# Products with T in seven half products in the FFN chunks of an attention kernel on one core

## The chip, the cores and the metric

The kernel runs on one core of a Trainium2 chip. Time is device microseconds of one launch; the kernel before has a median of 410.5 us over three runs (409.81 to 410.56).

## The reference

```
q_pool = q.reshape(B, H, S // 2, 2, D).mean(axis=3)          # B, H, S, D = 8, 8, 1152, 64
scores = 1 / sqrt(D) * q_pool @ k^T
attn   = softmax(scores)
x      = (attn @ v), heads side by side: 4608 tokens x 512
a, b   = x @ w1, x @ w2                                      # 512 x 1024 each
h      = a * b @ w3                                          # (a * b) @ w3, w3 is 1024 x 1024
out    = h @ w_out                                           # 1024 x 512
```

Since nothing stands between w3 and w_out, the kernel computes T = w3 @ w_out once (1024 x 512) and then (a * b) @ T. Matmuls take float16 and add up in float32; the output is float32.

## The kernel before, in words

**Attention.** The 64 heads go in 32 pairs; the score matrix of all pairs is cut into 324 slots of 512 columns for each head of a pair. A slot is one call of `scores` (L434): TensorE writes a buffer `psc` of two PSUM banks (three such buffers), ScalarE takes the exponential of it in one instruction (L448) into a ring of float16 in SBUF. Three slots make a visit, and there are 108 visits. The second product, probabilities by v, goes in 144 groups (`av_step`, L940; matmuls at L471 and L474), each for 128 pooled queries of one pair, or for the short last tiles of two pairs together. DVE divides by the sum of the row (L495 to L511), and the result is turned into `xT` by TensorE (first 8 pairs and short tiles, `x_turn`) or by a transposing DMA on SP's queue (`x_dma`, L481).

**Chunks of the FFN.** The 4608 tokens make 9 chunks of 512. For chunks 0 to 6 `moe_groups` (L597) yields fills, small portions of TensorE work that are put between the attention's. For each of 8 slices ft of d_ff there are two: the projection with w1 (kept in `asb` by DVE, L610) and that with w2, whose eviction multiplies with `asb` into `gT` (`gate`, L613). Then four fills of double length multiply 128 tokens each of gT with T (8 matmuls of 512 columns, L621); DVE scales the result into `osb` (L630), and a DMA stores it, on GpSimd's queue for chunks 0 to 4, on SP's for 5 and 6. T itself is made by earlier fills (`t_groups`, L544). A fill of length 1 is 8 matmuls of 256 columns or 4 of 512.

A fill writes either the one bank `mo` or one of the three psc buffers, which a slot of scores then has to wait for (`bank`, L536).

**The order.** Engines run their queues in the order of the program. Where fills, AV groups and turns of pairs stand between the visits is worked out when the kernel is built: `_visits` (L184) searches over sequences with a table of costs (`_Plan`, L115). In its sequences A is an AV group, P a turn of a pair, m and s a fill in `mo` or in a psc buffer. Chunk c is released to it once the AV groups that it needs are done (`loose`, L904). After the last visit the remaining AV groups and fills alternate (L985 to L992), with six PSUM banks instead of the psc buffers; then the rest of the fills runs without AV groups (L1013), with `asb` kept by ScalarE. Ahead of this loop, DVE has five small instructions for a check of the row sums (L1004 to L1010).

**Chunks 7 and 8** (`late_chunks`, L683) use Winograd's form of Strassen's method for all their products: a product of two matrices, each cut into 2 x 2 blocks, is made from 7 products of blocks instead of 8, with sums of blocks before and after. The sums of the left and right blocks are made by GpSimd: those of w1 and w2 (8 sums of 128 x 1024) and of T (4 of 128 x 1024) in one burst (`weight_sums`, L649, called at L971 when the last but one pair begins), those of x for chunks 7 and 8 (`x_sums`, L670) after the last AV group.

**GpSimd's queue** holds, per pair, the casts of k, q and v to float16 (`cast_kq`, `cast_v`, called by `prepare`, L878, two pairs ahead), the stores of most chunks, and loads of the first pairs. **SP's queue** holds the loads of later pairs, the transposing DMAs and the stores of chunks 5 and 6, in 24 pieces for the latter. At the start 33 matmuls on the identity (L859) run on TensorE before the first data is there.

Of the kernel before, what the change touches and what calls it, by code (L numbers as in the profile page):

```python
# [183 lines left out]
def _visits(n, start, units, pairs, fills, free, ready, width):  # L184
# [8 lines left out]
    for vis in range(n):  # L193
# [12 lines left out]
        def step(p, seq, na, f, pr, t0):  # L206
# [14 lines left out]
            if f < loose:  # L221
                for b in "ms":
                    q = p.copy()
                    q.fill(fills[f][0], fills[f][1], b == "s")
                    step(q, seq + b, na, f + 1, pr, t0)
# [40 lines left out]
def kernel(  # L266
# [26 lines left out]
    QM = 4  # L293
# [250 lines left out]
    def t_groups():  # L544
        w3T = {}

        def turn(ft):
            def go(pt):
                w3T[ft] = msb.tile([128, NF, 128], FP16, tag="w3T", bufs=2, name="w3T")
# [22 lines left out]
    CH = 512  # L572

# [22 lines left out]

    def moe_groups(c):  # L597
        t = {}

# [12 lines left out]
        for ft in range(NF):  # L612
            def gate(pb, ft=ft):  # L613
                nc.vector.tensor_tensor(out=t["g"][:, ft, :], in0=pb, in1=t["a"], op=ALU.mult)  # L614

            yield 1, lambda pa, ft=ft: first(pa, ft), keep, 0.0
            yield 1, lambda pb, ft=ft: proj(pb, w2sb, ft, c), gate, 0.0
        for tt in range(0, CH, 128):
            def go(po, tt=tt):
                for ft in range(NF):  # L620
                    nc.tensor.matmul(po, t["g"][:, ft, tt:tt + 128], T16[:, ft, :],  # L621
                                     start=(ft == 0), stop=(ft == NF - 1))

            def put(po, tt=tt):
                osb = msb.tile([128, dm], FP32, tag="osb", bufs=3)
                if tail[0]:
                    nc.vector.tensor_scalar_mul(out=osb[:, 0:256], in0=po[:, 0:256], scalar1=1.0 / (SCL * SCL))
                    nc.scalar.mul(out=osb[:, 256:512], in_=po[:, 256:512], mul=1.0 / (SCL * SCL))
                else:
                    nc.vector.tensor_scalar_mul(out=osb, in0=po, scalar1=1.0 / (SCL * SCL))  # L630
                if c == LATE - 1:
                    cut = 128 if tt < 256 else 64
                    for r in range(0, 128, cut):
                        for n in range(0, dm, 128):
                            store(nc.sync, c * CH + tt, osb[r:r + cut, n:n + 128], slice(n, n + 128), slice(r, r + cut))
                else:
                    store(nc.sync if c == LATE - 2 else nc.gpsimd, c * CH + tt, osb)

            yield 2, go, put, 0.0

    HF, HM, HC = NF // 2, dm // 2, CH // 2
    LATE = B * Sq // CH - 2
    IS = 1.0 / (SCL * SCL)
    wS, tS, xS = [], {}, {}
# [4 lines left out]
    def weight_sums():  # L649
        for w, tag in ((w1sb, "kst"), (w2sb, "vst")):  # L650
# [4 lines left out]
            nc.gpsimd.tensor_tensor(out=s1, in0=a21, in1=a22, op=ALU.add)  # L655
            minus(s2, s1, a11)
            minus(s3, a11, a21)
            minus(s4, a12, s2)
            wS.append({1: a11, 2: a12, 3: s4, 4: a22, 5: s1, 6: s2, 7: s3})
        b11, b12 = T16[:, 0:HF, 0:HM], T16[:, 0:HF, HM:dm]  # L660
        b21, b22 = T16[:, HF:NF, 0:HM], T16[:, HF:NF, HM:dm]
        st = [att.tile([128, 2, HF, HM], FP16, tag="qst", name="tS") for _ in range(2)]
        t1, t2, t3, t4 = st[0][:, 0], st[0][:, 1], st[1][:, 0], st[1][:, 1]
        minus(t1, b12, b11)
        minus(t2, b22, t1)
        minus(t3, b22, b12)
        minus(t4, b21, t2)
        tS.update({1: b11, 2: b21, 3: b22, 4: t4, 5: t1, 6: t2, 7: t3})

    def x_sums():  # L670
        st = msb.tile([128, 2, 4, NC // 2, HC], FP16, tag="wo", bufs=1, name="xS")
        for c in (0, 1):
            (_, a, n), = runs(LATE + c)
            b11, b12 = xT[:, 0:NC // 2, a:a + HC], xT[:, 0:NC // 2, a + HC:a + n]
            b21, b22 = xT[:, NC // 2:NC, a:a + HC], xT[:, NC // 2:NC, a + HC:a + n]
            x1, x2, x3, x4 = (st[:, c, i] for i in range(4))
            minus(x1, b12, b11)
            minus(x2, b22, x1)
            minus(x3, b22, b12)
            minus(x4, b21, x2)  # L680
            xS[c] = {1: b11, 2: b21, 3: b22, 4: x4, 5: x1, 6: x2, 7: x3}
# [149 lines left out]
    def fill(scored=False):  # L831
# [3 lines left out]
        pt = bank(scored) if put else None  # L835
        go(pt)
        if put:
            put(pt)
# [20 lines left out]
    for _ in range(33):  # L859
        nc.tensor.matmul(avb[:, 0:64], ident16, ident16[:, 0:64], start=True, stop=True)  # L860
# [60 lines left out]
    for ft in range(0, NF, 2):  # L921
        fills += [(0.5, W3_AT[ft // 2])] * 2 + [(1, WO_AT)] * 4
# [17 lines left out]
    def av_step():  # L940
# [9 lines left out]
        if p >= XD and t == QM - 1:  # L950
            x_dma(p)
        release()
# [46 lines left out]
    x_sums()  # L999
# [13 lines left out]
    while fill():  # L1013
        pass
    nc.tensor.matmul(avb[0:1, 0:1], okh, ones, start=True, stop=True)
# [39 lines left out]
```

## Time and profile before

| | |
|---|---|
| median of three runs | 410.5 us |
| the profiled execution | 411.45 us |
| its span, first to last instruction | 409.8 us |
| TensorE busy | 396.8 us, 97% |
| ScalarE busy | 335.2 us, 82% |
| DVE busy | 218.7 us, 53% |
| GpSimd busy | 212.8 us, 52% |
| end of the last exponential | 349.4 us |
| start of the late chunks on TensorE | 368.06 us |

Times in a profile are microseconds from the first instruction. PE is TensorE, PEld its weight loads (which overlap with matmuls), DVE VectorE, ACT ScalarE, POOL GpSimd, SP the engine that here only issues DMAs. A matmul's row covers its whole way through the array, so its duration is longer than the distance to the next one's start; distances of starts tell the rate. A row of the timeline is a run of equal instructions (xN), with the idle time of the engine ahead of it in brackets and what ended it.

### The profile page before, as it was taken

What the parts mean: (1) busy time and instruction counts of PE and PEld (TensorE: products, weight loads), DVE (VectorE), ACT (ScalarE), POOL (GpSimd) and SP (SyncE); (2) the same over time, 40 slices, a digit from 0 to 9 for tenths busy, and PEclk for the clock granted to TensorE, in tenths of its full rate; (3) what the DMA queues carried; (4) which work ended last, traced back from release to release, by engine and by line L of the source; (5) the groups of instructions that cost most, each with busy time, mean ns of one, the idle gap of its engine ahead of it and who ended that gap; (6) DMA issues with size and microseconds to landing.
All of it is one profiled execution on the core that took longest, in us unless ns stands there. A gap on an engine that the chain in (4) does not pass through costs nothing.

```text
span 409.8 us, 13190 instructions
## 1 busy us (share of the span) xinstructions
PE 396.8 (97%) x5506; PEld 261.6 (64%) x5506; DVE 218.7 (53%) x594; ACT 335.2 (82%) x380; POOL 212.8 (52%) x237
## 2 busy tenths in 40 slices
PE   5899999999999999999999999999999999999995
PEld 3477887565555655565556556655777655658884
DVE  1255565665355534654355536553546435765993
ACT  4978979898889998999989999999899889107752
POOL 5789966470664225504533336333633897051860
PEclk9999999999999999999999999999999999999999
DMA  8999999999598899949999999996998170121005
GB/s 278 251 308 268 274 289 304 346 238 292 173 265 228 198 283 249 260 114 248 245 277 261 250 304 255 259 321 144 278 241 180 26 151 19 22 62 50 9 26 183
DMA packets 94079, 86.35 MB, mean 211 GB/s; under 512 B 60096, under 2 KB 68544, under 8 KB 94016
## 3 DMA queue, kind: packets, MB, share of 16 engines
q1 hardware_dynamic: 84480, 60.11, 61.3%
q0 software_dynamic: 8384, 24.06, 21.1%
q10 hardware_dynamic: 1152, 1.31, 0.9%
q8 instruction: 43, 0.70, 0.7%
q14 instruction: 20, 0.16, 0.1%
HBM read 67.11 MB, written 9.44 MB: 187 GB/s over the span
## 4 chain that ended last, share of the span: by engine, by line
PE 88%; DMA 6%; POOL 2%; ACT 1%; issue 1%; DVE 1%; SPq 0%; ACTq 0%
PE psc L443 19%; PE avb L474 16%; PE mo L583 15%; PE mo L621 10%; PE mot L583 9%; PE b L724 7%; PE mo L561 3%; DMA qst<-in_q_dram 3%; PE avb L471 3%; DMA xT<-xb 3%; PE b L621 2%; PE mo L724 1%; PE ptk L383 1%; ACT ring L448 1%; DMA kst<-in_k_dram 1%; PE avb L724 1%
## 5 line engine op out<-in xcount | busy, mean ns | idle before, releaser
L448 ACT ACTIVATE ring<-psc 128x1024 f16<-128x1024 f32 x324 | 308.2, 1025 | 34.5 <-PE psc L443 32.7
L474 PEld LDWEIGHTS <-ring 128*128 128x128 f16 x2304 | 84.4, 98 | 26.3 <-issue 7.1
L443 PE MATMUL psc<-kqT 64*128 64x512 f16 (+7 forms) x1152 | 96.2, 290 | 3.6 <-ACT ring L448 0.9
L474 PE MATMUL avb<-vaug,ring 128*128 128x65 f16 x2304 | 91.4, 193 | 0.0
L355 POOL CAST kq<-kst 128x1152 f16<-128x1152 f32 x31 | 35.7, 1152 | 77.1 <-DMA kqT<-kq 52.9
L443 PEld LDWEIGHTS <-kqT 64*128 64x128 f16 x1152 | 45.8, 95 | 31.2 <-issue 8.5
L621 PE MATMUL mo<-T,gT 128*128 128x512 f16 x192 | 45.6, 380 | 0.0
L495 DVE RECIPROCAL rzall<-avb 128x2 f32<-128x2 f32 x144 | 23.8, 165 | 37.0 <-PE avb L474 20.3
L630 DVE TENSOR_SCALAR osb<-mo 128x512 f32<-128x512 f32 x24 | 16.6, 692 | 48.6 <-PE mo L621 48.6
L359 POOL TENSOR_TENSOR kq<-qst 128x512 f16<-128x512 f32 x31 | 39.4, 1272 | 1.1 <-DMA qst<-in_q_dram 1.1
L368 POOL CAST vaug<-vst 128x1152 f16<-128x1152 f32 x32 | 36.6, 1143 | 5.8 <-PE psc L443 5.3
L595 POOL DMA_DIRECT2D out_dram<-osb x18 | 9.9, 552 | 55.9 <-DVE rzall L495 55.9
L614 DVE TENSOR_TENSOR gT<-mo,asb 128x512 f16<-128x512 f32 x36 | 24.9, 692 | 24.7 <-PE mo L583 24.4
L583 PE MATMUL mo<-xT,w2sb 128*128 128x512 f16 (+2 forms) x168 | 37.2, 350 | 0.0
L621 PEld LDWEIGHTS <-gT 128*128 128x128 f16 x224 | 19.8, 98 | 25.5 <-issue 5.2
L610 DVE COPY asb<-mo 128x512 f32<-128x512 f32 x32 | 22.1, 691 | 25.2 <-PE mo L583 24.9
L583 PEld LDWEIGHTS <-w2sb 128*128 128x128 f16 x256 | 21.9, 97 | 20.8 <-issue 4.2
L583 PEld LDWEIGHTS <-w1sb 128*128 128x128 f16 x256 | 22.0, 97 | 20.4 <-issue 3.9
L583 PE MATMUL mo<-xT,w1sb 128*128 128x512 f16 (+2 forms) x148 | 33.3, 351 | 1.1 <-DMA xT<-xb 1.1
L509 DVE TENSOR_TENSOR xb<-avb,rzall 128x128 f16<-128x128 f32 x96 | 28.0, 291 | 3.3
L583 PE MATMUL mot<-xT,w1sb 128*128 128x512 f16 (+1 forms) x104 | 23.6, 354 | 0.1
L583 PE MATMUL mot<-xT,w2sb 128*128 128x512 f16 (+1 forms) x84 | 19.5, 359 | 0.0
(143 smaller groups left out, 432.7 us busy)
## 6 DMA issues: line engine op xcount, KB each, us to landing
vst<-in_v_dram SPq DMA_DIRECT2D x25, 576.0 KB, 5.0
kst<-in_k_dram SPq DMA_DIRECT2D x23, 576.0 KB, 5.8
qst<-in_q_dram SPq DMA_DIRECT2D x23, 512.0 KB, 7.3
kst<-in_k_dram POOLq DMA_DIRECT2D x8, 576.0 KB, 9.9
out_dram<-osb POOLq DMA_DIRECT2D x18, 256.0 KB, 6.1
qst<-in_q_dram POOLq DMA_DIRECT2D x8, 512.0 KB, 10.6
vst<-in_v_dram POOLq DMA_DIRECT2D x7, 576.0 KB, 6.9
w3c<-in_moe_w_dram POOLq DMA_DIRECT2D x4, 512.0 KB, 8.2
```

The lines of the kernel that those rows point to most:

```text
L355: nc.gpsimd.tensor_copy(out=kq16[:, 0:NJ].rearrange("p c u d -> p u c d"), in_=kst.rearrange("p u (c d) -> p u c d", d=D))
L359: eng.tensor_tensor(out=kq16[:, NJ:NJ + QM].rearrange("p c u d -> p u c d"), in0=qv[:, :, :, 0], in1=qv[:, :, :, 1], op=ALU.add)
L368: nc.gpsimd.tensor_copy(out=va[:, :, :, 0:D], in_=vs.pop(p).rearrange("p u (c d) -> p u c d", d=D))
L443: nc.tensor.matmul(psc[:, u, f - s * G:f - s * G + ln], kT2[u * 64:u * 64 + 64, jt, :], qpT[u * 64:u * 64 + 64, i0:i0 + ln], start=True, s ...
L448: nc.scalar.activation(out=ring[:, :, r0:r0 + G], in_=psc, func=AF.Exp, bias=0.0, scale=SCALE)
L474: nc.tensor.matmul(avb[:, o + u * E1:o + u * E1 + E1], ring[:, u, c0:c0 + 128], va[:, u, jt, :], start=(jt == 0 and u == 0), stop=(jt == N ...
L495: nc.vector.reciprocal(out=rzall[:, i, :], in_=av[:, :, D:E1].rearrange("p u o -> p (u o)"))
L509: nc.vector.tensor_tensor(out=xbt, in0=av[:, :, 0:D], in1=rzall[:, i, :].unsqueeze(2).to_broadcast([128, 2, D]), op=ALU.mult)
L583: nc.tensor.matmul(pw[:, d0:d0 + n], wt[:, mc, ft * 128:ft * 128 + 128], xT[:, mc, a:a + n], start=(mc == 0 and d0 == 0), stop=(mc == NC - ...
L614: nc.vector.tensor_tensor(out=t["g"][:, ft, :], in0=pb, in1=t["a"], op=ALU.mult)
L621: nc.tensor.matmul(po, t["g"][:, ft, tt:tt + 128], T16[:, ft, :], start=(ft == 0), stop=(ft == NF - 1))
L724: nc.tensor.matmul(pt[:, n * f:n * f + n], l[:, i, :], b[:, i, :], start=(p in (1, 5) and f == 0 and i == 0), stop=(i == kc - 1), skip_gro ...
```

## The change

For chunks 0 to 6 the product of gT (512 x 1024) with T (1024 x 512) is done in the seven-product form too. A product P1 to P7 is one fill of normal length: 8 matmuls of 256 columns for two 128-token tiles and 4 slices of d_ff. The left blocks' sums are three GpSimd operations in gT itself and one new buffer `s1` (`sums`): for the first two slices together, behind the gate of ft 5, then for one slice each, behind the gates of ft 6 and 7; a fourth sum, in two operations, follows behind P2. P1 stands as a fill between ft 4 and ft 5. The other six are held in `late_fills` and come behind the first two fills of the next chunk (LAG = 2); for chunk 6 they come at once. In the order P2, P6, P7, P4, P5, P3, DVE adds up the parts into the four quarters of the output (256 tokens x 256 columns); P3 adds into the bank of P5 after P5 was read, so it takes no bank of its own. The planner gets P5 and P3 as fills for `mo` alone.

So a chunk has 23 fills of length 1 instead of 16 of length 1 and 4 of length 2, and 23 evictions instead of 20. A quarter is stored with one DMA of two tiles where the rows allow it (`store_two`), else two or three; on GpSimd's queue for chunks 0 to 5, and on SP's, in 32 pieces, for chunk 6.

The sums of T move into chunk 0, one behind each of the first four gates. The sums of w1 and w2 come one behind each AV group from the last but one pair on. The x sums of chunk 8 move behind the last fill of chunk 6; those of chunk 7 stay after the last AV group. Buffers are shared anew (T sums take that of w_out, x sums those of q), and the 33 matmuls at the start are gone.

```diff
-        for tt in range(0, CH, 128):
-            def go(po, tt=tt):
-                for ft in range(NF):
-                    nc.tensor.matmul(po, t["g"][:, ft, tt:tt + 128], T16[:, ft, :],
-                                     start=(ft == 0), stop=(ft == NF - 1))
...
-            yield 2, go, put, 0.0
+        def product(pt, a, n, start=True):
+            for u in range(2):
+                for f in range(HF):
+                    nc.tensor.matmul(pt[:, u * HM:u * HM + HM], a[:, f, u * 128:u * 128 + 128], tS[n][:, f, :],
+                                     start=(start and u == 0 and f == 0), stop=(f == HF - 1), skip_group_check=True)
+
+        def plus(out, pt, x):
+            nc.vector.scalar_tensor_tensor(out=out, in0=two(pt), scalar=IS, in1=x, op0=ALU.mult, op1=ALU.add)
+
+        def quarter(h, n, pt, x):
+            osb = msb.tile([128, 2, HM], FP32, tag="osb", bufs=3, name="osb")
+            plus(osb, pt, x)
+            if c < LATE - 1:
+                store_two(nc.gpsimd, c * CH + h * HC, osb, slice(n * HM, n * HM + HM))
+                return
+            for u in range(2):
+                for r in range(0, 128, 64):
+                    for o in range(0, HM, 128):
+                        store(nc.sync, c * CH + h * HC + u * 128, osb[r:r + 64, u, o:o + 128],
+                              slice(n * HM + o, n * HM + o + 128), slice(r, r + 64))
...
+        def sums(f, n):
+            g = t["g"]
+            if f == 0:
+                t["s1"] = msb.tile([128, HF, HC], FP16, tag="s1", bufs=1, name="s1")
+            fs = slice(f, f + n)
+            s1, a11, a21, a22 = t["s1"][:, fs], g[:, fs, 0:HC], g[:, fs, HC:CH], g[:, HF + f:HF + f + n, HC:CH]
+            nc.gpsimd.tensor_tensor(out=s1, in0=a21, in1=a22, op=ALU.add)
+            minus(a21, a11, a21)
+            minus(a11, s1, a11)
+
+        def half(fts):
+            for ft in fts:
+                def gate(pb, ft=ft):
+                    nc.vector.tensor_tensor(out=t["g"][:, ft, :], in0=pb, in1=t["a"], op=ALU.mult)
+                    if c == 0 and ft < HF:
+                        t_sum(ft)
+                    if ft > HF:
+                        sums(*((0, 2) if ft == HF + 1 else (ft - HF, 1)))
+
+                yield 1, lambda pa, ft=ft: first(pa, ft), keep, 0.0
+                yield 1, lambda pb, ft=ft: proj(pb, w2sb, ft, c), gate, 0.0
+                if 2 * ft + 2 == LAG:
+                    yield from lagged
+
+        yield from half(range(HF + 1))
+        yield 1, lambda pt: product(pt, t["g"][:, 0:HF, 0:HC], 1), p1, 0.0
+        yield from half(range(HF + 1, NF))
...
+        late_fills.extend((
+            (1, lambda pt: product(pt, g[:, HF:NF, lo], 2), p2, 0.0),
+            (1, lambda pt: product(pt, g[:, 0:HF, lo], 6), lambda pt: plus(t["p"], pt, t["p"]), 0.0),
+            (1, lambda pt: product(pt, g[:, 0:HF, hi], 7), p7, 0.0),
+            (1, lambda pt: product(pt, g[:, HF:NF, hi], 4), lambda pt: quarter(1, 0, pt, t["z"]), 0.0),
+            (1, p5, lambda pt: quarter(1, 1, pt, t["z"]), 0.0),
+            (1, lambda pt: product(t["bank"], g[:, HF:NF, lo], 3, False),
+             lambda pt: quarter(0, 1, t["bank"], t["p"]), None),
+        ))
+        if c == LATE - 1:
+            yield from late_fills
+            late_fills.clear()
...
+    def weight_sum():
+        if todo:
+            o, x, y, op = todo.pop(0)
+            nc.gpsimd.tensor_tensor(out=o, in0=x, in1=y, op=op)
...
-    for _ in range(33):
-        nc.tensor.matmul(avb[:, 0:64], ident16, ident16[:, 0:64], start=True, stop=True)
...
-            fills += [(1, 0.0)] * (2 * NF) + [(2, 0.0)] * (CH // 128)
+            step = [(1, 0.0, "ms")]
+            rest = step * 4 + [(1, 0.0, "m")] * 2
+            fills += step * LAG + (rest if c else []) + step * (2 * NF + 1 - LAG) + (rest if c == LATE - 1 else [])
...
         if p >= XD and t == QM - 1:
             x_dma(p)
+        weight_sum()
         release()
...
-    x_sums()
+    x_sums(0)
...
     while fill():
         pass
+    x_sums(1)
```

More of the change, by code (lines that the diff above doesn't have):

```diff
@@ new lines, in p1 @@
+        def p1(pt):
+            t["p"] = msb.tile([128, 2, HM], FP32, tag="t2k", bufs=2, name="p")
+            nc.vector.tensor_scalar_mul(out=t["p"], in0=two(pt), scalar1=IS)
+        def sums(f, n):
[7 more added lines that the diff above has]
+            minus(a11, s1, a11)
@@ new lines, in moe_groups, with p2, p7 @@
+        yield from half(range(HF + 1))
+        yield 1, lambda pt: product(pt, t["g"][:, 0:HF, 0:HC], 1), p1, 0.0
+        yield from half(range(HF + 1, NF))
+        g = t["g"]
+        lo, hi = slice(0, HC), slice(HC, CH)
+        def p2(pt):
+            quarter(0, 0, pt, t["p"])
+            for f in range(0, HF, 2):
+                minus(g[:, HF + f:HF + f + 2, lo], g[:, HF + f:HF + f + 2, lo], g[:, f:f + 2, lo])
+        def p7(pt):
+            t["z"] = msb.tile([128, 2, HM], FP32, tag="t2k", bufs=2, name="z")
+            plus(t["z"], pt, t["p"])
@@ new lines, in p5 @@
+        def p5(pt):
+            t["bank"] = pt
+            product(pt, t["s1"], 5)
+        late_fills.extend((
[7 more added lines that the diff above has]
+        ))
@@ new lines, in x_sums @@
+    def x_sums(c):
+        st = att.tile([128, 4, NC // 2, HC], FP16, tag="qst", name="xS")
+        (_, a, n), = runs(LATE + c)
+        b11, b12 = xT[:, 0:NC // 2, a:a + HC], xT[:, 0:NC // 2, a + HC:a + n]
+        b21, b22 = xT[:, NC // 2:NC, a:a + HC], xT[:, NC // 2:NC, a + HC:a + n]
+        x1, x2, x3, x4 = (st[:, i] for i in range(4))
+        minus(x1, b12, b11)
+        minus(x2, b22, x1)
+        minus(x3, b22, b12)
+        minus(x4, b21, x2)
+        xS[c] = {1: b11, 2: b21, 3: b22, 4: x4, 5: x1, 6: x2, 7: x3}
@@ L921 @@
     for ft in range(0, NF, 2):
[L922 removed]
+        fills += [(0.5, W3_AT[ft // 2], "ms")] * 2 + [(1, WO_AT, "ms")] * 4
     free = []
```

82 lines of the change are left out of this document (30 added, 52 removed).

## The prediction

> **What bounds the kernel now.** I read the page first, then busy time by 10 us windows, then the timeline of single stretches, then the groups kept apart by shape.
>
> The page: busy time per engine, and the chain that ended last.
>
> ```profile
> PE 396.8 (97%) x5506; PEld 261.6 (64%) x5506; DVE 218.7 (53%) x594; ACT 335.2 (82%) x380; POOL 212.8 (52%) x237
> ...
> PE 88%; DMA 6%; POOL 2%; ACT 1%; issue 1%; DVE 1%; SPq 0%; ACTq 0%
> ```
>
> TensorE is the bound, and nearly everything on the chain is its own work. GpSimd has 197 us idle. The windows (busy us per engine, count in brackets) say where:
>
> ```profile
> 300.00:310.00 10.00, 10.00 (x178) 7.86 (x176) 4.93 (x16) 9.58 (x11) 3.01 (x4) 1.00 1.00 233
> 320.00:330.00 10.00, 9.88 (x148) 6.33 (x145) 3.96 (x12) 9.22 (x11) 9.92 (x5) 1.00 0.27 62
> 350.00:360.00 10.00, 10.00 (x168) 6.27 (x165) 7.81 (x23) 0.00 (x0) 1.47 (x2) 1.00 0.08 16
> 380.00:390.00 10.00, 10.00 (x94) 8.97 (x92) 9.40 (x13) 7.14 (x14) 9.16 (x8) 1.00 0.02 6
> ```
>
> First column: TensorE; the fifth: GpSimd, which is full only where the weight and T sums run (320 to 345). From 380, 94 matmuls of 256 columns take 10 us, so 0.1064 us each. One visit, on TensorE and ScalarE:
>
> ```profile
> 102.58 1.90 PE L621 MATMUL mo<-T,gT 128*128 128x512 f16 x8
> 104.32 0.71 PE L474 MATMUL avb<-vaug,ring 128*128 128x65 f16 x18
> 104.87 0.22 PE L516 MATMUL avb<-ident,xbt 128*128 128x128 f16 x1
> 105.02 0.83 PE L443 MATMUL psc<-kqT 64*128 64x512 f16 x10
> ...
> 105.51 2.85 ACT L448 ACTIVATE ring<-psc 128x1024 f16<-128x1024 f32 x3 [0.34 <-PE psc L443]
> ```
>
> Starts give the prices: a product of 8 matmuls 1.74, an AV group 0.55, its turn 0.15, three score slots 0.76, together 3.20. ScalarE needs 2.85 per visit and waits 0.34 for TensorE. So a visit shrinks with its matmul work, but not below 2.85. After the last visit (348.62) the rest of the AV groups and fills run without exponentials until the late chunks start:
>
> ```profile
> 360.41 1.89 PE L621 MATMUL b<-T,gT 128*128 128x512 f16 x8
> 362.14 0.71 PE L474 MATMUL avb<-vaug,ring 128*128 128x65 f16 x18
> 362.69 5.34 PE L621 MATMUL b<-T,gT 128*128 128x512 f16 x24
> ...
> 368.06 0.61 PE L724 MATMUL b<-xT,w1sb 128*128 128x256 f16 x4
> ```
>
> No wait: the products of chunk 6 need only the gates. The GpSimd price of a sum, three of them in a row:
>
> ```profile
> 359.65 1.16 POOL L647 TENSOR_TENSOR xS<-xT 128x512 f16<-128x512 f16 x1
> 360.76 1.15 POOL L647 TENSOR_TENSOR xS<-xT,xS 128x512 f16<-128x512 f16 x1
> 361.87 1.15 POOL L647 TENSOR_TENSOR xS<-xT 128x512 f16<-128x512 f16 x1
> ```
>
> 1.11 us from start to start for 512 elements per partition. The weight sums of 1024 start 2.09 us apart (mean 2.13); through these two points a sum of 256 takes 0.62, which I use. Half of 1.11 is 0.56, and the slowest row of a 512 sum (1610 ns at L814, late chunks) would make it 0.85: these are the ends.
>
> **Part by part, against the profiled execution** (span 409.8, time 411.45; its time is 0.95 above the median 410.5, so differences are added to the median).
>
> *The product itself.* Per chunk 32 matmuls of 512 columns become 56 of 256: 4 x 1.74 = 6.96 against 7 x 0.866 = 6.06. Over seven chunks 6.2 us less TensorE work. How much comes back depends on the order, which I take from the two instruction orders. There are 108 visits in both. Before, they hold 135 AV groups and 152 of 164 fills; after, 137 and 165 of 185. I priced a visit by its content with the mean distance of the starts of visits in the timeline of ScalarE (every third exponential).
>
> *Visits 20 to 106* take 273.4 us now. After: 37 visits of an AV group and two single fills at 3.18; 13 of the same with a turn at 3.26; 18 of two AV groups and a single fill at 2.90; 5 with a tail group at 2.94 (the same shape now, without one visit of 4.20 whose fill waited 1.1 us for a transfer of xT; after, that fill comes two AV groups later); 8 of other known shapes, 25.1; 6 lighter ones that have no row, at the 2.85 floor or what they add to it, 17.7. Sum 269.7: **-3.6**. With 4.20 kept it is -2.6.
>
> *Visits 0 to 19* take 65.8 us. After, they hold three fills and one AV group less (3 x 0.87 + 0.7 = 3.3). Visit by visit with the nearest shapes (3.0 for two AV groups and a fill with turns, 3.4 where a pair is turned, 2.87 where only one fill is left) I get 62.8: **-3.0**, between -1.5 (transfers decide here) and -3.3.
>
> *Between the visits and the late chunks* 19.44 us now. After: one fill, then 7 AV groups with 7 fills at 1.41 (349.48 to 350.89), 0.35 for the tail group and turn, then 12 fills at 0.866, 0.1 for the check: 21.6: **+2.1**. So without any wait the change would give -4.5.
>
> *The last chunk's wait.* This decides. Call 0 the start of the sixth ft (ft 5) of chunk 6; what is left on TensorE is ft 5, 6, 7, then P2, P6, P7, P4, P5, P3, all back to back. Their gates, from P1's eviction (DVE, to 0.9) and the five small check instructions that now stand ahead of the gate (1.70 from 365.22 to 366.92): gate 5 done at 3.3; gates 6 and 7 at 4.4 and 6.1 (5.2 end of the projection + 0.2 + 0.69). GpSimd runs its x sums for chunk 7 before that (they wait for the turn of the last short tile, as at 358.54 now, and end about at 0). Then: three sums of 512 from 3.35 to 6.7, three of 256 to 8.5, three more to 10.4. P2 needs none and ends at 6.07. P6 needs all of them: it can issue its first three matmuls, then stands until 10.4. It ends at 11.0; P7, P4, P5 to 13.55. P3 adds into the bank of P5 and waits for P5's eviction (0.2 + 0.69), so it runs 14.5 to 15.35 instead of ending at 10.4. **+4.9** (ends: 0.56 per small sum and the check instructions out of the way +3.9; 0.85 and 1.61 +7.5). Everything behind it in TensorE's queue is late by that: the late chunks follow at full rate (94 matmuls in 10 us) and give nothing back. P3's eviction needs the output buffer of the first quarter: 8 stores on SP at 0.66 (20 in 13.21) from 7.0 to 12.3, landing 1.9: 14.2, in time. SP's 32 stores end before the late chunks' first store, which comes some 22 us after their start.
>
> *Chunks 0 to 5.* There the lag (two fills of the next chunk and P2) stands between the last gate and P6, some 5 us. GpSimd's queue there also holds the casts (1.15 + 1.27 + 0.45 + 1.14 = 4.0 per pair) and the stores. By its instruction order the last sums are done 1.7 to 2.2 us before P6 in chunks 0, 2, 3, 4, 5 us before in chunk 1. In chunk 5 a cast and three weight sums (1.15 + 3 x 2.09) stand ahead of its last three sums: these end 11.4 us after visit 101 starts, and P6's fourth matmul comes at 10.95: **+0.5**, 0 to 2. The fourth quarter's output buffer waits for the store of the first: 0.73 issue (a two-part load's row) + 6.1 landing against 9 us: no wait in the mean, but POOL late by a cast would make one, and DVE's gates and normalizations stand behind it. For that and for 185 evictions in place of 164 on the few banks I take **+0.5** (0 to 4).
>
> *Hidden.* GpSimd gets 5 x 1.11 + 6 x 0.62 = 9.3 us of sums per chunk, 65 us, out of 197 idle, and the stores of chunk 5 from SP (8 issues of 0.55); the four T sums (2.13 each) move from 337 to chunk 0, where GpSimd has 5 us idle in 10. DVE gets 3 x 0.69 per chunk, 14.5 us, of 191 idle. If this cover is gone, P6 or a gate shows it: the second rival.
>
> *The 33 warm-up matmuls.* They end at 3.4 us; the first real one starts at 4.70 on a cast, so they hide nothing directly. Do they speed up what follows?
>
> ```profile
> 14.70 1.65 PE L383 MATMUL ptk<-ident,kq 128*128 128x128 f16 x14 [0.31 <-ACT ring L448]
> ...
> 25.53 0.95 PE L383 MATMUL ptk<-ident,kq 128*128 128x128 f16 x14
> ```
>
> The same 14 turns take 1.65 us at 14.7 and 0.95 at 25.5, so TensorE still runs at half rate eleven us after the warm-up; it had no effect to lose. **0** (0 to +0.5). The windows' granted clock shows 1.00 in both stretches, so it doesn't carry this.
>
> The Trainium skill ("TensorE: Matmul & The Clock Gate", Part 1) says that the array drops to half rate after an idle window of about 3.4 us and needs as long a busy one to recover. The slow start agrees; that a wait inside the kernel does it, no stretch of this trace shows, since the longest after the start is 1.1 us.
>
> **Sum:** -3.6 - 3.0 + 2.1 + 4.9 + 0.5 + 0.5 = +1.4, so 411.9 (412.85 for an execution like the profiled one).
>
> **Rivals.**
> *The end doesn't wait long.* Without the 4.9 the time is 407.0, and it is faster by more than 0.2% (0.8 us) as long as TensorE stands less than 2.7 us at P6 and P3 together. For it: all other parts are gains. Against: nine sums follow gate 5 in one queue and need 7 us, while TensorE has 4.3 us of work left before P6. Time 407 to 409.7, taking 408.5. Chance 0.27.
> *GpSimd's queue is late in every chunk.* The margin before P6 is 2 us in four chunks, and one cast is 4.0. If a cast there finds its input late (casts wait 52.9 us now for the turn of the pair before, in ten waits), P6 stands for it, by 1 to 2 us in each of four chunks: +4 to +6, 416.5. Against: these waits come from GpSimd running ahead, which it no longer can. Decides if the casts ahead of the last sums start over 2 us after the visit they belong to. Chance 0.2.
> *TensorE slows after the wait.* If the 4 us stand at the end puts it at half rate, the 37 matmuls to P3's end take 0.107 more each: +3.9, 415.8. For it the half rate until about 18 us, where TensorE had gaps of 0.3 to 1.3; against, the wait is broken by three matmuls. The rule of the page named above would give this. Chance 0.08.
> *As forecast:* 411.9, own range 409.5 to 413.5; chance 0.45.
>
> **Chances and range.** A difference under 0.2% can hardly be measured here. Faster: 0.25 of the first rival and 0.02 of the forecast, 0.27. Within 0.2% (409.7 to 411.3): 0.02 and 0.13, 0.15. Slower: 0.30 of the forecast and the other two, 0.58. The range goes from the first rival's middle down one us, 407.5, to the second's price, 416.5.
>
> **What would show it.** Right: visits 20 to 106 in about 270 us; in the waits TensorE's loads for P6 on GpSimd's sums of gT, once, about 3.5 us, some 6 us after the last AV group's fills, and one of P3 on DVE, 0.9; the late chunks as long as now (41.7 us). Wrong: several such waits in 80 to 330 us (the second rival), P6 behind P2 without a gap (the first), P7 to P3 with 0.21 us between matmuls (the third), or visits that are not shorter.

## The result and the profile after

The changed kernel takes 416.11 us (median; 415.84 to 416.49) against 410.53 before (four runs of each): a ratio of 1.0134, 95% interval [1.0121, 1.0146], so 5.6 us slower where 1.4 was forecast. Its profiled execution took 415.84 us with a span of 414.0. The two profiled executions differ by 4.4 only, since the one before stood 0.9 above its median and this one 0.3 below.

Three marks from the timelines of the two profiled executions place the difference. The last is the start of the last group of matmuls, which ends TensorE's work; what follows it is the landing of the last stores, 5.5 us before and 4.7 after in these two executions. That is why the spans differ by 4.2 and TensorE's work by 4.95.

| TensorE | before | after | change | forecast |
|---|---|---|---|---|
| first fill after the last visit starts | 348.62 | 343.80 | -4.8 | -5.6 |
| from there to the late chunks | 19.44 | 29.20 | +9.8 | +7.0 |
| late chunks, first to last group of matmuls | 36.25 | 36.26 | 0 | 0 |
| sum | | | +4.95 | +1.4 |

The visits gave what the change was said to take out of them, nearly; the stretch behind them took twice that back. The page of the changed kernel, with busy time per engine and the chain that ended last:

```profile
PE 393.6 (95%) x5641; PEld 277.7 (67%) x5641; DVE 232.3 (56%) x612; ACT 335.8 (81%) x381; POOL 291.4 (70%) x330
...
PE 86%; POOL 5%; ACT 4%; DVE 2%; issue 1%; DMA 1%; ACTq 0%; POOLq 0%
```

TensorE is busy for 3.2 us less, and ends its work 4.95 us later. GpSimd, which had 2% of the chain, now has 5%. The windows (length, then busy us and count for TensorE, its weight loads, DVE, ScalarE and GpSimd, then granted clock, DMA share and GB/s) say where:

```profile
320.00:330.00 10.00, 10.00 (x189) 7.42 (x186) 5.37 (x18) 9.52 (x11) 9.30 (x9) 1.00 0.45 75
350.00:360.00 10.00, 10.00 (x99) 5.73 (x96) 7.40 (x22) 1.60 (x3) 7.48 (x8) 1.00 0.24 67
360.00:370.00 10.00, 5.92 (x33) 3.73 (x32) 2.77 (x4) 0.16 (x1) 9.53 (x12) 0.83 0.10 26
380.00:390.00 10.00, 10.00 (x94) 8.98 (x92) 9.14 (x14) 6.87 (x14) 4.94 (x4) 1.00 0.16 41
367.00:369.00 2.00, 2.00 (x11) 1.43 (x10) 0.69 (x1) 0.00 (x0) 2.00 (x3) 0.50 0.19 49
```

From 360 to 370 TensorE is busy for 5.92 us, with 33 matmuls, while GpSimd is full; and the granted clock, 1.00 elsewhere, is 0.50 in the middle of it. The late chunks run at 94 matmuls in 10 us as before. TensorE's timeline through that stretch:

```profile
360.24 0.49 PE L632 MATMUL b<-T,gT 128*128 128x256 f16 x3
361.26 0.72 PE L632 MATMUL b<-T,gT 128*128 128x256 f16 x5 [0.53 <-DVE gT L670]
361.93 0.39 PE L632 MATMUL b<-tS,gT 128*128 128x256 f16 x2
364.04 0.28 PE L632 MATMUL b<-tS,gT 128*128 128x256 f16 x1 [1.72 <-POOL gT L716]
366.15 4.13 PE L632 MATMUL b<-tS,gT 128*128 128x256 f16 x21 [1.83 <-POOL gT L716]
370.12 1.04 PE L632 MATMUL b<-tS,s 128*128 128x256 f16 x8
371.94 1.03 PE L632 MATMUL b<-T,gT 128*128 128x256 f16 x8 [0.78 <-DVE osb L636]
373.00 0.61 PE L794 MATMUL b<-xT,w1sb 128*128 128x256 f16 x4
```

P2 waits 0.53 us for the last gate. P6 issues three matmuls with waits of 1.72 and 1.83 for GpSimd. Then 21 matmuls take 4.13 us: 16 of them, those that start from 366.28 to 369.48, are each followed by the next after 0.21 us, and the others after 0.11 to 0.12. P3 waits 0.78 for the eviction of P5. And GpSimd, on whose sums P6 waits:

```profile
358.25 1.15 POOL L663 TENSOR_TENSOR s<-gT 128x512 f16<-128x512 f16 x1 [2.35 <-DVE gT L670]
359.49 1.15 POOL L716 TENSOR_TENSOR gT<-gT 128x512 f16<-128x512 f16 x1
360.72 1.16 POOL L716 TENSOR_TENSOR gT<-s,gT 128x512 f16<-128x512 f16 x1
...
363.94 0.67 POOL L663 TENSOR_TENSOR s<-gT 128x256 f16<-128x256 f16 x1
364.69 0.67 POOL L716 TENSOR_TENSOR gT<-gT 128x256 f16<-128x256 f16 x1
365.43 0.67 POOL L716 TENSOR_TENSOR gT<-s,gT 128x256 f16<-128x256 f16 x1
```

The nine sums run without a pause from the gate of ft 5, in three groups of three. Within a group they start 1.23 us apart for the large ones and 0.745 for the small; the first sum of the next group starts 1.11 and 0.62 after the one before it, as two sums do that don't need each other. Within a group each reads or overwrites what the one before it touched.

From the start of ft 5 (355.06) to the late chunks it is 17.94 us, for 10.5 us of TensorE's work: 7.4 us of stand and slow running where 4.9 was forecast. Two questions follow, and the runs were chosen for them. Is the stretch of half rate caused by the wait, and would it go if TensorE had work? And how much of the loss is GpSimd's being too slow for the last chunk, against a change in the rest of the kernel that costs something too (fewer visits saved than forecast, the missing warm-up, the weight sums spread out)?

### The profile page after: what moved, and what is told of

Its sections match the earlier page's. It is cut to its first block, busy times and chain, and to the rows that moved or that the text cites. A ratio compares the mean times of both kernels' runs of the same rounds, so it can differ in the third digit from the quotient of the medians.

```text
span 414.0 us, 13566 instructions
## 1 busy us (share of the span) xinstructions
PE 393.6 (95%) x5641; PEld 277.7 (67%) x5641; DVE 232.3 (56%) x612; ACT 335.8 (81%) x381; POOL 291.4 (70%) x330
## 4 chain that ended last, share of the span: by engine, by line
PE 86%; POOL 5%; ACT 4%; DVE 2%; issue 1%; DMA 1%; ACTq 0%; POOLq 0%
PE psc L443 19%; PE avb L474 17%; PE mo L587 12%; PE mot L587 9%; PE b L794 6%; PE mo L632 6%; ACT ring L448 3%; PE mo L561 3%; PE mot L632 3%; PE avb L471 2%; POOL gT L716 2%; PE b L632 2%; PE ptk L383 2%; POOL wS L731 2%; PE mo L794 1%
## 5 line engine op out<-in xcount | busy, mean ns | idle before, releaser
L443 PE MATMUL psc<-kqT 64*128 64x512 f16 (+7 forms) x1152 | 98.0, 291 | 5.1 <-ACT ring L448 2.2
L443 PEld LDWEIGHTS <-kqT 64*128 64x128 f16 x1152 | 46.8, 95 | 34.7 <-issue 13.1
L663 POOL TENSOR_TENSOR s<-gT 128x256 f16<-128x256 f16 (+1 forms) x21 | 17.4, 828 | 42.1 <-DVE gT L670 32.7
L632 PEld LDWEIGHTS <-gT 128*128 128x128 f16 x336 | 31.5, 100 | 16.0 <-POOL gT L716 5.2
L716 POOL TENSOR_TENSOR gT<-gT 128x512 f16<-128x512 f16 (+1 forms) x35 | 33.3, 963 | 1.8
L587 PE MATMUL mot<-xT,w1sb 128*128 128x512 f16 (+1 forms) x124 | 27.8, 351 | 0.0
L627 DVE COPY asb<-mo 128x512 f32<-128x512 f32 x25 | 17.3, 692 | 16.6 <-PE mo L587 16.3
L587 PE MATMUL mo<-xT,w1sb 128*128 128x512 f16 (+1 forms) x116 | 25.9, 351 | 0.0
L627 DVE COPY asb<-mot 128x512 f32<-128x512 f32 x27 | 18.7, 692 | 5.0 <-PE mot L587 5.0
L716 POOL TENSOR_TENSOR gT<-s,gT 128x256 f16<-128x256 f16 (+1 forms) x21 | 17.4, 830 | 1.6
```

Source lines behind the costliest of these rows:

```text
L443: nc.tensor.matmul(psc[:, u, f - s * G:f - s * G + ln], kT2[u * 64:u * 64 + 64, jt, :], qpT[u * 64:u * 64 + 64, i0:i0 + ln], start=True, s ...
L587: nc.tensor.matmul(pw[:, d0:d0 + n], wt[:, mc, ft * 128:ft * 128 + 128], xT[:, mc, a:a + n], start=(mc == 0 and d0 == 0), stop=(mc == NC - ...
L627: nc.vector.tensor_copy(out=t["a"], in_=pa)
L632: nc.tensor.matmul(pt[:, u * HM:u * HM + HM], a[:, f, u * 128:u * 128 + 128], tS[n][:, f, :], start=(start and u == 0 and f == 0), stop=(f ...
L716: nc.gpsimd.tensor_tensor(out=out, in0=x, in1=y, op=ALU.subtract)
```

## The experiments

Each ratio is to the kernel before, run on the same chip. All edits but one are made in the changed kernel.

**The last chunk as it was.** Chunk 6 goes back to its four fills of double length; chunks 0 to 5 keep the seven products.

```diff
-                    if ft > HF:
+                    if ft > HF and c < LATE - 1:
                         sums(*((0, 2) if ft == HF + 1 else (ft - HF, 1)))
...
+        if c == LATE - 1:
+            yield from half(range(NF))
+            for tt in range(0, CH, 128):
...
+                yield 2, go, put, 0.0
+            return
         yield from half(range(HF + 1))
...
```

> Chunk 6 alone goes back to the four double fills of 8 matmuls of 512 columns, with evictions on DVE and ScalarE as before the change; chunks 0 to 5 stay in seven half products. Theory A: both waits and the slow stretch at the end go (1.72 + 1.83 + 0.53 + 1.7 + 0.78 = 6.6 us), TensorE gets 0.9 us more work: 410.4, about the time before the change or a little faster. Rival B (loss spread over the visits): the end gives back little, 414 to 416.

409.81 us, ratio 0.9972 [0.9959, 0.9985]: faster than before. TensorE's timeline at the end of chunk 6 shows no wait:

```profile
358.48 1.03 PE L587 MATMUL b<-xT,w2sb 128*128 128x512 f16 x4
359.34 7.07 PE L686 MATMUL b<-T,gT 128*128 128x512 f16 x32
366.44 0.61 PE L816 MATMUL b<-xT,w1sb 128*128 128x256 f16 x4
```

The late chunks start at 366.44 instead of 373.00, 6.56 us earlier. That is the 7.4 of the waits less the 0.9 that chunk 6's own product saves, so the whole loss is in the last chunk, and the rest of the change gains.

**TensorE kept busy.** 34 matmuls of 256 columns, whose result nothing reads, stand between P2 and P6 of chunk 6.

```diff
             quarter(0, 0, pt, t["p"])
+            if c == LATE - 1:
+                for _ in range(34):
+                    nc.tensor.matmul(avb[:, 0:256], ident16, T16[:, 0, 0:256], start=True, stop=True)
             for f in range(0, HF, 2):
```

> 34 matmuls of 256 columns on the identity into a bank that nothing reads stand between P2 and P6 of chunk 6 (3.6 us of TensorE work, less than the 4 us that it stands there); GpSimd's sums stay. Theory A1 (the 16 matmuls at half rate behind the wait come from TensorE standing idle): the wait for GpSimd is as long as before, but the matmuls behind it are 0.107 us apart; 16 x 0.107 = 1.7 us come back, 414.4. Rival A2 (they are slow for another cause, such as GpSimd's sums reading the same tile): still 0.213 apart, 416.1 or a little more.

414.72 us, ratio 1.0091 [1.0069, 1.0112]. TensorE's timeline from the added matmuls on:

```profile
361.93 3.88 PE L691 MATMUL avb<-T,ident 128*128 128x256 f16 x34
365.64 3.10 PE L632 MATMUL b<-tS,gT 128*128 128x256 f16 x24
368.57 1.04 PE L632 MATMUL b<-tS,s 128*128 128x256 f16 x8
...
371.45 0.61 PE L797 MATMUL b<-xT,w1sb 128*128 128x256 f16 x4
```

24 matmuls in 3.10 us, of which 0.3 is a last wait of P6: full rate right after the sums' end, and the late chunks start 1.55 us earlier, although TensorE did 34 matmuls more. The half rate was caused by the stand, and in this pair of executions it costs about 1.6 us. The sums that P6 waits for end as late as before, so the rest of the loss should be theirs; the next runs test that.

**The nine sums on DVE.** In chunk 6 alone, DVE makes the sums behind the gates.

```diff
-            nc.gpsimd.tensor_tensor(out=s1, in0=a21, in1=a22, op=ALU.add)
-            minus(a21, a11, a21)
-            minus(a11, s1, a11)
+            eng = nc.vector if c == LATE - 1 else nc.gpsimd
+            eng.tensor_tensor(out=s1, in0=a21, in1=a22, op=ALU.add)
+            eng.tensor_tensor(out=a21, in0=a11, in1=a21, op=ALU.subtract)
+            eng.tensor_tensor(out=a11, in0=s1, in1=a11, op=ALU.subtract)
```

> The nine sums of chunk 6 go from GpSimd to DVE; all else stays. In the changed kernel TensorE stands 1.72 + 1.83 us at P6 for these sums, then issues 16 matmuls 0.213 us apart instead of 0.107 (366.16 to 369.48), then stands 0.78 us at P3. Theory A (the end of chunk 6 is what the change loses: the wait for GpSimd, and the slow matmuls that follow from it): DVE makes a sum of 512 in 0.4 us (its row in the late chunks), so P6's last wait shrinks to 1.0 to 1.5 us, too short to slow TensorE; 416.1 falls by 4.0 to 5.5, to 410.6 to 412.1, and no matmul distance of 0.213 is left there. Rival B (the loss is spread over the visits, through GpSimd's fuller queue): under 1 us comes back, 415.1 or more.

413.43 us, ratio 1.0069 [1.0047, 1.0091]: better, but short of what was expected. The half rate is gone, and P6's wait is 0.89; but two new things came. TensorE's timeline has both waits:

```profile
363.49 2.47 PE L632 MATMUL b<-tS,gT 128*128 128x256 f16 x21 [0.89 <-DVE gT L666]
...
371.54 0.60 PE L795 MATMUL avb<-xT,w1sb 128*128 128x256 f16 x4 [1.81 <-DVE badi L1089]
```

DVE's timeline, at the last sums and at the last eviction:

```profile
361.86 0.29 DVE L665 TENSOR_TENSOR gT<-gT 128x256 f16<-128x256 f16 x1
362.18 1.25 DVE L666 TENSOR_TENSOR gT<-s,gT 128x256 f16<-128x256 f16 x1
...
370.74 0.69 DVE L636 SCALAR_TENSOR_TENSOR osb<-b,p 128x512 f32<-128x512 f32 x1 [3.18 <-DMA out_dram<-osb]
```

And GpSimd's:

```profile
362.14 1.15 POOL L717 TENSOR_TENSOR gT<-gT 128x512 f16<-128x512 f16 x1 [6.54 <-PE b L632]
```

The last small sum takes 1.25 us instead of 0.29. In these 1.25 us GpSimd runs the first half of the fourth sum (362.14 to 363.29), and DVE's sum ends 0.14 behind it. That is P6's 0.89. The second: the fourth quarter's eviction waits 3.18 us for its output buffer, whose first quarter is being stored in 8 pieces on SP's queue. Behind it in DVE's queue stands an instruction of the check, and TensorE's third late unit waits 1.81 us for that. In the changed kernel the last eviction finds its buffer free. There P2's eviction, which starts this store, came 7.0 us after ft 5 and the last eviction 18.0; here P2's stands behind the sums on DVE, at 8.6, and P3 is done sooner.

**The fourth quarter in place.** On top of the sums on DVE, the fourth quarter of chunk 6 is added up in `p` and stored from there, so it needs no output buffer.

```diff
-            osb = msb.tile([128, 2, HM], FP32, tag="osb", bufs=3, name="osb")
+            last = c == LATE - 1 and (h, n) == (0, 1)
+            osb = x if last else msb.tile([128, 2, HM], FP32, tag="osb", bufs=3, name="osb")
```

> As e1_dve_sums, but the fourth quarter of chunk 6 is added up in the buffer that it adds to and stored from there, so its eviction needs no output buffer. In e1 DVE waited 3.18 us there for the store of the first quarter, with the last instruction of the check behind it, and TensorE's third unit of the late chunks waited 1.81 us for that. Theory (this wait took the place of part of the one removed, and it stands on TensorE's queue): the 1.8 us come back, 411.6 against 413.4. Rival (the late chunks would have lost this time anyway to the sums of chunk 8, which GpSimd makes at the same time): 413.0 or more, with another wait in its place.

412.01 us, ratio 1.0031 [1.0014, 1.0048], and the wait of 1.81 is gone; the eviction now waits for its own matmuls alone:

```profile
368.97 0.69 DVE L636 SCALAR_TENSOR_TENSOR p<-b,p 128x512 f32<-128x512 f32 x1 [1.12 <-PE b L632]
```

So the second of the two was the buffer. Two runs tried the first, both on top of this kernel.

**The fourth sum written behind P6's eviction.**

```diff
             quarter(0, 0, pt, t["p"])
+            if c < LATE - 1:
+                fourth()
+
+        def p6(pt):
+            plus(t["p"], pt, t["p"])
+            if c == LATE - 1:
+                fourth()
...
```

> As e9_in_place, and the fourth sum of chunk 6 on GpSimd comes behind P6's eviction, not behind P2's. In e1 DVE's last small sum took 1.25 us instead of 0.29, while GpSimd made a sum of 512 (1.15 us, from 362.14) over the same 1.1 us, and P6 waited 0.89 us for it. Theory (two-input operations on both engines hold each other up): with nothing on GpSimd at that time the small sum takes 0.29 us again, P6's wait shrinks to almost nothing, and 0.9 us come back against e9, 410.7. Rival (the small sum is slow for another reason, such as its operands): 1.25 us again, no change against e9.

411.69 us, ratio 1.0021 [1.0009, 1.0032]: within the interval of the run before it. The edit changed nothing of what it aimed at: later in the program is not later on GpSimd, which waits for P2 only and started that sum at 362.75, again beside DVE's last one (362.80, 1.25 us). This run tells nothing of the cause.

**Its two halves in the other order.** The half that starts first now overwrites what DVE's last sum reads, so GpSimd has to wait for DVE.

```diff
-            for f in range(0, HF, 2):
+            for f in ((2, 0) if c == LATE - 1 else (0, 2)):
                 minus(g[:, HF + f:HF + f + 2, lo], g[:, HF + f:HF + f + 2, lo], g[:, f:f + 2, lo])
```

> As e9_in_place, with the two halves of chunk 6's fourth sum on GpSimd in the other order: the first now needs the sums that DVE makes last, so GpSimd can't work while DVE does. (In e10_in_place_fourth the sum was written behind P6's eviction, but nothing in it waits for that, and GpSimd still ran it from 362.75 over DVE's last small sum, which took 1.25 us again.) Theory (two-input operations on SBUF on both engines exclude each other): DVE's last small sum takes 0.29 us, P6's wait falls from 0.89 to about 0, and 0.9 us come back against e9: a ratio of 1.001 to the kernel before, 411.1. Rival (slow by its operands): 1.25 us and 0.89 us as before.

410.51 us, ratio 0.9994 [0.9982, 1.0006]. DVE's last sums, then TensorE:

```profile
361.87 0.29 DVE L666 TENSOR_TENSOR gT<-gT 128x256 f16<-128x256 f16 x1
362.20 0.29 DVE L667 TENSOR_TENSOR gT<-s,gT 128x256 f16<-128x256 f16 x1
```

```profile
361.57 0.72 PE L632 MATMUL b<-T,gT 128*128 128x256 f16 x5 [1.13 <-DVE gT L672]
362.12 2.89 PE L632 MATMUL b<-tS,gT 128*128 128x256 f16 x24
```

0.29 us, and P6 no longer waits. With the same instructions and only their overlap taken away, DVE's sum takes a quarter of the time: GpSimd's addition had held it up. What is left is P2's wait of 1.13 for the last gate, which now has sums ahead of it on DVE, and P3's 0.78. With these, chunk 6 in seven products is still no better than an ordinary one: 0.9994 [0.9982, 1.0006] here, 0.9972 [0.9959, 0.9985] there.

**The weight sums later.** Where the changed kernel makes them, they cost chunk 5's P6 a wait of 0.69 us. TensorE, changed kernel:

```profile
333.97 0.72 PE L632 MATMUL mot<-tS,gT 128*128 128x256 f16 x5 [0.69 <-POOL gT L716]
```

Here they begin after the 136th AV group.

```diff
     def weight_sum():
-        if todo:
+        if todo and avn[0] > 135:
```

> In the changed kernel the eight weight sums start only with the 136th AV group, behind chunk 5's sums, still one behind each group. TensorE stood 0.69 us at chunk 5's P6 in the changed kernel (at 333.97), with three weight sums of 2.1 us ahead of these sums in GpSimd's queue. Theory (the weight sums cause this wait, and the engine is saturated there): the wait goes and 0.5 to 0.7 us come back, 415.4 to 415.6. Rival (the later weight sums run into the x sums and the sums of chunk 6 and lengthen the wait at the end): as much or more is lost there, 416 to 419.

421.96 us, ratio 1.0278 [1.026, 1.0296]: the rival was right. The 0.69 is gone, but everything behind them on GpSimd is late. GpSimd still makes weight sums until 359.2 and x sums until 363.9, and chunk 6's sums run from 363.91 to 371.76. Chunk 6's gates are late too, for the reason that the next run shows, but P2 has its last one at 362.25, before these sums begin. TensorE:

```profile
367.58 0.61 PE L632 MATMUL b<-tS,gT 128*128 128x256 f16 x2 [4.09 <-POOL gT L716]
369.70 0.40 PE L632 MATMUL b<-tS,gT 128*128 128x256 f16 x1 [1.51 <-POOL gT L716]
371.82 4.33 PE L632 MATMUL b<-tS,gT 128*128 128x256 f16 x21 [1.72 <-POOL gT L716]
```

The late chunks start 7.1 us after the end of the last sum; in the changed kernel it was 6.9. This confirms from the other side that the end goes by when GpSimd comes free.

**The same delay with an ordinary chunk 6**, where GpSimd has no sums to be late with.

```diff
+        if c == LATE - 1:
+            yield from half(range(NF))
+            ...
...
-        if todo:
+        if todo and avn[0] > 135:
```

> e5_plain_last (chunk 6 with the product of the kernel before) with the weight sums from the 136th AV group on, as in e6. Here no sums of chunk 6 stand behind them. Theory (0.69 us at chunk 5's P6 go, nothing new comes): 409.1 to 409.3, faster than the kernel before by 0.3% and the fastest so far. Rival (the weight sums delay the x sums of chunk 7, which the late chunks need): 409.8 or more, with a wait for xS behind the start of the late chunks.

411.42 us, ratio 1.0019 [1.0006, 1.0032]: a miss; the ordinary chunk 6 alone had 0.9972. The five check instructions on DVE now run beside the weight sums. DVE, then GpSimd, then TensorE:

```profile
354.81 2.23 DVE L1100 TENSOR_SCALAR ok<-rzall 128x288 f32<-128x288 f32 x1
357.07 2.26 DVE L1101 TENSOR_TENSOR ok<-ok 128x288 f32<-128x288 f32 x1
```

```profile
354.69 2.19 POOL L753 TENSOR_TENSOR wS<-w2sb 128x1024 f16<-128x1024 f16 x1
356.83 2.18 POOL L753 TENSOR_TENSOR wS<-w2sb,wS 128x1024 f16<-128x1024 f16 x1
```

```profile
360.68 0.39 PE L686 MATMUL b<-T,gT 128*128 128x512 f16 x1 [1.43 <-DVE gT L670]
```

In the changed kernel, with GpSimd idle, the same two DVE instructions take 0.30 and 0.46 us:

```profile
356.08 0.30 DVE L1075 TENSOR_SCALAR ok<-rzall 128x288 f32<-128x288 f32 x1
356.42 0.46 DVE L1076 TENSOR_TENSOR ok<-ok 128x288 f32<-128x288 f32 x1
```

In this run each starts during a sum and ends with one, 0.16 and 0.32 us behind it. The gates behind them are late, and TensorE waits 1.43 and some smaller times. It is the effect of the DVE sums once more, on other instructions and other buffers.

**The weight sums a little later, the check behind the gates.** An ordinary chunk 6, the weight sums from after the 132nd AV group, and six fills issued ahead of the check.

```diff
-        if todo:
+        if todo and avn[0] > 131:
...
     x_sums(0)
 
+    for _ in range(6):
+        fill()
     NQ = NU * 2
```

> As e5_plain_last; the weight sums begin with the 132nd AV group (behind chunk 5's sums, but four groups earlier than in e8), and DVE's check instructions come six fills later. In e8_plain_later two of them, on SBUF alone, took 2.23 and 2.26 us instead of 0.30 and 0.46 beside weight sums on GpSimd, and the gates behind them made TensorE wait 1.43 + 0.21 + 0.41 us. Theory: neither wait is left, neither the 0.69 us at chunk 5's P6: 0.7 us less than e5, a ratio of 0.9955 to the kernel before. Rival (GpSimd's work just moves on, and the x sums or check instructions meet it later): no better than e5's 0.9972, with a wait behind 358 us.

408.99 us, ratio 0.995 [0.9934, 0.9966]: faster than the kernel before and than the changed one, and the fastest of all. No wait of TensorE after 30 us is over 0.4, and the late chunks start at 365.16, 2.9 us before the 368.06 of the kernel before. GpSimd still meets the check: beside x sums of 1.20 and 1.22 us the same two DVE instructions take 1.26 and 1.29. But no gate stands behind them any more, and TensorE doesn't wait for them. What the six fills do by themselves was not tried.

```profile
365.06 0.16 PE L1113 MATMUL avb<-ones,okh 128*1 128x1 f16 x1
365.16 0.61 PE L816 MATMUL b<-xT,w1sb 128*128 128x256 f16 x4
```

**The warm-up.** The 33 matmuls go back into the changed kernel.

```diff
+    for _ in range(33):
+        nc.tensor.matmul(avb[:, 0:64], ident16, ident16[:, 0:64], start=True, stop=True)
     for t in kq16s:
```

> The 33 matmuls at the start are put back into the changed kernel. In the profiles TensorE's rate doubles at 18.9 us before and at 21.5 us after the change; visit 4 starts 1.1 us later after. Theory of the prediction (they have no effect, the start differs by chance and by the other order of the visits): 416.1, within 0.4. Rival (the earlier work brings the full rate earlier): the rate doubles at about 18.9 again and 0.5 to 1.1 us come back, 415.0 to 415.6.

416.89 us, ratio 1.0143 [1.0121, 1.0165], no different from the changed kernel's 1.0134 [1.0121, 1.0146]. TensorE reaches its full rate at 19.2 us instead of 21.5 and visit 4 starts 0.6 earlier, but visit 7 starts at 30.62 against 30.67 and visit 20 at 71.56 against 71.61. At the end of chunk 6 the waits are those of the changed kernel, but in this execution the granted clock was 0.50 for 6.83 us (363.96 to 370.79) instead of 3.41, and from ft 5 to the late chunks it took 0.6 us longer. So the price of the half rate differs from one execution to another.

**The kernel before without its warm-up.**

```diff
-    for _ in range(33):
-        nc.tensor.matmul(avb[:, 0:64], ident16, ident16[:, 0:64], start=True, stop=True)
     for t in kq16s:
```

> The kernel before without the 33 matmuls at the start: that one part of the change alone. With them put back into the changed kernel, TensorE's rate doubled at 19.2 instead of 21.5 us and visit 4 began 0.6 us earlier, but visit 7 at the same time. Theory (the full rate comes one window of 3.4 us later at most, and the waits of the first visits for the loads of w3 take it up): the same as before within 0.2%, 410.2 to 411.5, and visit 20 within 0.5 us of 73.2. Rival (it costs what half rate costs over 2.6 us of work): 1.3 us more, 411.8 to 412.4.

411.18 us, ratio 1.0019 [0.9992, 1.0047]: no difference that can be told. Visit 20 was 1.0 us later here, more than the 0.5 expected, but a wait of 1.06 for xT at 205 us was absent and visit 104 started at 336.88 against 337.11. What was lost early came back before the end.

## Why the forecast was too low

By the steps of the prediction:

- *Visits 20 to 106*, -3.6: right. From visit 20 to visit 104 the changed kernel gains 3.89 us (starts of exponentials: 73.23 to 337.11 before, 71.61 to 331.60 after); to the start of visit 107, where the term ends, it gains 3.26, with the wait of chunk 5's P6 in it. The forecast for these two together was -3.1. Pricing each visit by the mean of visits of equal content held.
- *Visits 0 to 19*, -3.0: too much. Visit 20 starts 1.62 us earlier, near the bound of -1.5 given for the case that transfers decide there. Up to visit 7 (30.64 and 30.67) nothing is gained; all of the 1.62 comes after. What holds the first seven visits was not tried; the warm-up isn't it, as putting it back changes visit 20 by 0.05. The timeline has one candidate. At 28.33 the changed kernel's scores wait 0.77 us for DVE's copies of `kqT`, where the kernel before has a fill between the turns and the scores and no wait.
- *The warm-up*, 0: right, as both runs show.
- *Chunk 5's P6*, +0.5: measured 0.69, by the weight sums ahead of it, as worked out. *Other waits*, +0.5: between 30 and 330 us TensorE has none over 0.4 us, so GpSimd's queue was late nowhere else and the second rival falls.
- *Between the visits and the late chunks*, +2.1: right. From the first fill after the last visit to ft 5 of chunk 6 it took 11.26 us where 11.1 was in the sum.
- ***The last chunk's wait*, +4.9, is the step that failed in size: 7.4.** Its mechanism was right in every part. GpSimd's nine sums follow the gate of ft 5, P6 issues three matmuls and stands, P3 waits 0.78 for P5 (0.9 in the working), and nothing behind gives anything back. Two sizes were wrong. The sums' distance was taken from sums that don't wait for the one just before, 1.11 as read and 0.62 as worked out from it, where within their groups these had 1.23 and 0.745; the last one ended 11.04 us after the start of ft 5 instead of 10.4: +0.64. And the array ran at half rate after the wait: 16 matmuls 0.104 us too long each, +1.7; the forecast put this at nothing. What is left of the 2.5, about 0.2, I can't place.
- *TensorE slows after the wait* was put down as a rival to the forecast with a chance of 0.08. It was no alternative: it came on top of it, and its price of 3.9, for 37 matmuls, was too high, as the half rate ended after 16. The argument against it, that three matmuls break the wait, was wrong. That it ended after 16 isn't fixed either: in the execution with the warm-up put back the half rate held for two stretches of 3.41 us.

The two add up: 0.8 us less gained in the visits than forecast, 2.76 more lost behind them, together the 3.55 by which TensorE's end missed the forecast. The direction was right and the median lies just inside the range, but outside the forecast's own range of 409.5 to 413.5.

One cover was thin. The prediction let the fourth quarter find its output buffer free "in time", 14.2 us after ft 5 with P3 ending at 15.35. In the changed kernel it did, as P3 ran 17 us after ft 5. With the sums on DVE, P2's eviction came later, P3 sooner, and the same store cost 1.81.

The Trainium skill ("TensorE: Matmul & The Clock Gate", Part 1) gives the half rate as what follows an idle window of about 3.4 us, with as long a busy one to recover, the windows running free of the program. This case agrees in the main: the granted clock was 0.50 from 366.26 to 369.67, 3.41 us. It also shows that the window needn't be wholly idle: in the 3.41 us ahead of 366.26 TensorE was busy for 0.39 us, and ahead of the half rate in the runs with the warm-up put back and with the weight sums later for 1.21 and 1.27.

## What to carry to other kernels

A change that moves work from the bound engine to an idle one pays where something stands between the two (here the lag of two fills in chunks 0 to 5) and costs where the work ends in a straight line, however idle the helper is on average; the last pass of a loop may deserve the old form. Price a chain of dependent instructions by dependent ones, and add to any stretch of some 3.4 us in which TensorE mostly stands what it runs slower afterwards: the remedy for that part can be as cheap as matmuls that nobody reads. And before GpSimd is given a burst of additions, look at which DVE additions and scalings from SBUF to SBUF fall into it and who waits for them.

## What was not expected of the hardware

- DVE's TENSOR_TENSOR and TENSOR_SCALAR with all operands in SBUF stretched to the end of a GpSimd addition that ran beside them: 0.29 to 1.25 us beside one of 1.15, 0.30 to 2.23 and 0.46 to 2.26 beside those of 2.19. The run with the fourth sum's halves exchanged shows that the overlap makes it. Not every instruction on SBUF is hit: the check's TENSOR_REDUCE took 0.45 us beside an x sum (359.37 in the run with the same delay and an ordinary chunk 6) as without one. DVE's evictions from PSUM took 0.69 us with and without GpSimd beside them. The Trainium skill ("GPSIMD Engine Reference", "8. Key points") says that GpSimd shares its SBUF interfaces with DVE and contends with its two-input and fast modes. These runs agree and put a size on it: DVE loses the rest of the GpSimd instruction, not a share of its rate.
- The half rate came and went in steps of 3.41 us. In the changed kernel it held for one step, in the run with the warm-up put back for two, and in the run with the late weight sums for four (13.65 us from 362.01, that is from before the stand of 4.09). It ended each time behind a step in which TensorE was busy throughout. A step with 1.27 us of TensorE's work was enough to bring it on; in the run with the sums on DVE a step with 1.6 (368.72 to 372.13, counted from the first change of the clock on record) brought none. Where the steps fall differs between executions, so a wait of the same length can cost or not.
- At the start, TensorE reached full rate at 18.9 us before and 21.5 after, although it was busy for 67% and 54% of the first 18 us. The 33 matmuls need not be the reason: in the profiles of the eleven kernels without them the granted clock stays at 1.00 from between 18.9 and 21.9 us, and no effect of them on the end was seen.
